# The half split behind the router, the last tile's chain first, and 15 warm-up matmuls in a fused attention, mixture-of-experts and SoLU kernel

## The chip, the cores and the metric

One core of a Trainium2 chip runs the whole program in one launch. The metric is the device time of one execution, in microseconds, as the median of several runs. An instruction belongs to one of five engines with a queue of its own: TensorE (PE: matmuls, with PEld for its weight loads), VectorE (DVE), ScalarE (ACT), GpSimd (POOL) and SyncE (SP, which issues transfers). Each engine takes its instructions in program order, and they wait for one another through semaphores.

## The reference

Three parts follow one another. The first is a gated linear attention with a stabilised recurrence, for 2 batches of 8 heads, 768 steps and head width 40:

```
m_new = max(f + m, i);  f_s = exp(f + m - m_new);  i_s = exp(i - m_new)
C = f_s * C + i_s * v k^T;   n = f_s * n + i_s * k
y = sigmoid(o) * (C q) / max(|n . q|, 1)
```

Its output is 1536 tokens of width 320. The second part sends each token to two of eight experts:

```
noisy = x @ w_gate + log1p(exp(x @ w_noise)) * noise
top2  = the two largest of noisy;  weights = softmax over the two
out  += weight * (relu(x @ w1[e]) @ w2[e])          # 320 -> 1024 -> 320
```

The third is a dense layer: h = x @ w_in, a softmax over h times h, a layer norm with gain g_ln, and a product with w_out (320 to 1024 to 320).

## The kernel before

**Stages.** The tokens are 12 tiles of 128; the batches alternate (`order`). Stage 1 (to about line 800) is the attention in chunks of 128 steps together with the routing. Then come the experts one after the other, and then the SoLU layer. Matrix products of the experts run as sums of a high part, rounded to the fast matmul format, and a low part, the remainder: for each weight ACT makes the high part (`split_hi`, L116) and DVE or POOL subtracts it from the raw weight (`split_lo`, L120).

**Order.** The schedule is manual: the order in which the program is written is the order on each engine. `weave` takes several short chains of DVE steps and writes one step of each in turn.

**The head.** `gates(0, 1)` (L268 to L285) runs two scans on DVE for the first chunk. G holds the sums of the log gates. Its high part goes to rows 0 to 15 of GP (L281), its low part to rows 32 to 47 (L282). `sel` (L297) is a selection matrix taken from the constants, in the fast format. `decays` multiplies sel by GP on PE (tile D, L307). Ahead of that, 20 matmuls of 448 columns on a constant tile `warm` (L253) keep PE busy; they write pw. Meanwhile POOL clears buffers (L240). ACT computes the sigmoid of the first two output gates (og_s, L298).

**A round of the loop** (i = 4 to 10, L678 to L717) works on four tiles at once. PE: ranks of tile i-3 (L452), scores of i+1 (tile S, L343), update of the state with i (tile U, L371), the part of i that goes through the state (L379), attend of i (tile Y, L384), transposes of i-1 (`trans`, tile pT, L418) and the router's logits (L428). DVE: the weave, made of `rows(i-1)` (normalise, x, L404 to L408; copy, L412), `route(i-2)` (top two of the noisy logits, one-hot oh, mask mk, running counts cum, L441 to L448) and `slot(i-3)` (row of each token in the experts' buffer, L458 to L460); then `probs` (E times S, L347, two halves), `keys` (kw, L360) and `state` (CC, L394). ACT: exponentials, and copies of pT (`transc`, L422). POOL: `send(i-3)` scatters the tile's tokens to their experts' rows in memory (xg, L476, an indirect transfer, two for each tile), then the causal mask on E (`causal`, L336), the queries' weighting (qa, L353) and the state's (CC, L355). From i = 5 on, DVE makes in each round one half of one of expert 0's first three low weights: w0l = r - w0h, 128x512, L703, **the half split**, behind probs(i+1, 1) and ahead of the next weave.

**The tail** (L722 to L798) handles tile 11, which is t. The first 192 rows of expert 0 are final by then, and the program starts on them: `early_turn` transposes them (ept, L506), `early_split` makes their high and low parts, `early_mm(f)` is layer 1 for one block of 128 hidden columns, eight matmuls (eph, L126 to L133). `split2(j)` makes one more low weight on DVE (L120) and loads another (r). `busy(n)` writes n matmuls on `warm`, as the warm-ups. When the last tile is sent, SP loads the rest of expert 0's rows (`rest`), and the expert stage turns them (L924).

Of the kernel before, what the change touches and what calls it, by code (L numbers as in the profile page):

```python
# [8 lines left out]
F32 = mybir.dt.float32  # L9
# [12 lines left out]
P = 128  # L22
# [14 lines left out]
def fused_kernel(ctx: ExitStack, tc, qt, kt, kv, og, ig, fg, wgn, noise, w1, w2, win, wout, gln, cst, out):  # L37
# [157 lines left out]
    with ExitStack() as pa:  # L195
# [53 lines left out]
            ve.memset(Kb[0][j], 0.0)  # L249
        ve.memset(Qb[0], 0.0)  # L250
        pw = ps1.tile([P, 512], F32, tag="U", name="pw")
        for i in range(20):
            pe.matmul(pw[:, 0:448], warm[:, 0:P], warm, start=True, stop=True)  # L253

        def fill(n, tag="U"):
# [12 lines left out]
        def gates(c0, c1):  # L268
            lo, hi = c0 * P, c1 * P
            m0, m1 = M[:, lo:hi], M[:, lo + 1 : hi + 1]  # L270
            Fs, Is, Gs = F[:, lo:hi], I[:, lo:hi], G[:, c0:c1].rearrange("p c t -> p (c t)")
            yield ve.tensor_tensor_scan(m1, Fs, Is, -1e30 if c0 == 0 else M[:, lo : lo + 1], ALU.add, ALU.max)
            if c0 == 0:
                ve.tensor_sub(M[:, 0:1], M[:, 1:2], F[:, 0:1])
            yield ve.tensor_add(Fs, Fs, m0)
            yield ve.tensor_sub(Fs, Fs, m1)
            yield ve.tensor_tensor_scan(Gs, R1[:, 0 : c1 - c0].rearrange("p c t -> p (c t)"), Fs, 0.0, ALU.mult, ALU.add)
            if c1 > 2:
                act.dma_start(gd[:, max(2, c0) * P : hi], G[:, max(2, c0) : c1].rearrange("p c t -> p (c t)"))
            if c0 < 2:  # L280
                yield ve.tensor_copy(GP[0:16, c0], G[:, c0])  # L281
                yield ve.tensor_sub(GP[32:48, c0], G[:, c0], GP[0:16, c0].bitcast(F32))  # L282
            yield ve.tensor_sub(Is, Is, m1)
            yield ve.tensor_sub(Is, Is, Gs)
            yield ve.tensor_add(BE[:, c0:c1], Iv[:, c0:c1], G[:, c0:c1, P - 1 : P].to_broadcast([16, c1 - c0, P]))  # L285
# [6 lines left out]
            ve.tensor_copy(bT[:, c0:c1], pb[:, 0, c0:c1])  # L292
            act.activation(wS[:, c0:c1], pb[:, 1, c0:c1], AF.Exp)

        for k, _ in enumerate(gates(0, 1)):
            if k == 3:
                ve.tensor_copy(sel, consts[0:48, 2 * P + 24 : 2 * P + 40])  # L297
        act.activation(og_s[:, 0:2], og_s[:, 0:2], AF.Sigmoid)  # L298
        act.preload_act_table_set("natural_log_exp_and_others")

# [80 lines left out]
        def attend(i, lo=0, hi=NH):  # L381
            b, c = order[i]
            for h in range(lo, hi):
                pe.matmul(T[i]["Y"][:, h], T[i]["E"][:, h], values(i)[:, h], start=(c == 0 and h == 0), stop=(h == NH - 1))  # L384
# [13 lines left out]
        def rows(i):  # L398
            Y = T[i]["Y"]
            den = a2.tile([P, NH, 1], F32, tag="den", name=f"den{i}")  # L400
            nm = a2.tile([P, NH, HD], F32, tag="nm", name=f"nm{i}")
            xx = T[i]["x"] = a4.tile([P, XR + 1], F32, tag="x", name=f"x{i}")
            pool.tensor_copy(xx[:, 384:385], tokid[:, i : i + 1])
            yield ve.tensor_scalar(den, Y[:, :, 40:41], -1.0, 1.0, op0=ALU.mult, op1=ALU.max)  # L404
            yield ve.tensor_mul(nm, Y[:, :, 0:HD], og_s[:, i].rearrange("p (h d) -> p h d", d=HD))
            yield ve.tensor_max(den, den, Y[:, :, 40:41])
            yield ve.reciprocal(den, den)
            yield ve.tensor_mul(xx[:, 0:DM].rearrange("p (h d) -> p h d", d=HD), nm, den.to_broadcast([P, NH, HD]))  # L408

        def rows2(i):  # L410
            xx = T[i]["x"]
            yield ve.tensor_copy(xx[:, DM:384], xx[:, 256:DM])  # L412

        def trans(i):
            pT = T[i]["pT"] = ps1.tile([P, 4, P], F32, tag="pT" if i < NTILE - 1 else "U", name=f"pT{i}")
            for k in range(3):
                w = min(P, DM - k * P)
                pe.transpose(pT[:w, k], T[i]["x"][:, k * P : k * P + w], ident)  # L418

        def transc(i):  # L420
            xT = T[i]["xT"] = a2.tile([P, 3, P], F32, tag="xT", name=f"xT{i}")
            act.activation(xT[:, 0:2], T[i]["pT"][:, 0:2], AF.Copy)  # L422
            act.activation(xT[0:64, 2], T[i]["pT"][0:64, 2], AF.Copy)
# [11 lines left out]
        def route(i):  # L435
            z = T[i]["z"]
            ix = a2.tile([P, 8], U32, tag="ix", name=f"ix{i}")
            ixf = T[i]["x"][:, 385:387]
            oh = T[i]["oh"] = a2.tile([P, 2, NE], F32, tag="oh", name=f"oh{i}")
            mk = T[i]["mk"] = a2.tile([P, NE], BF16, tag="mk", name=f"mk{i}")  # L440
            yield ve.tensor_mul(z, T[i]["pT"][:, 3, 32:40], noise_s[:, i])  # L441
            yield ve.tensor_add(z, z, T[i]["pT"][:, 3, 0:8])
            yield ve.max(V8[:, i], z)
            yield ve.max_index(ix, V8[:, i], z)
            yield ve.tensor_copy(ixf, ix[:, 0:2])
            yield ve.tensor_tensor(oh, ixf.rearrange("p (k o) -> p k o", o=1).to_broadcast([P, 2, NE]), iota8.rearrange("p (k e) -> p k e", k=1).to_broadcast([P, 2, NE]), op=ALU.is_equal)
            yield ve.tensor_add(mk, oh[:, 0], oh[:, 1])
            yield ve.tensor_add(cum[i + 1], cum[i], mk)  # L448
# [6 lines left out]
        def slot(i):  # L455
            sk = a2.tile([P, 2, NE], F32, tag="sk", name=f"sk{i}")
            sf = a2.tile([P, 2], F32, tag="sf", name=f"sf{i}")
            yield ve.tensor_mul(sk, T[i]["oh"], T[i]["pr"].rearrange("p (k e) -> p k e", k=1).to_broadcast([P, 2, NE]))  # L458
            yield ve.tensor_reduce(sf, sk, axis=AX.X, op=ALU.add)
            yield ve.tensor_copy(slots[:, i], sf)  # L460

        def weave(*chains):

            chains = list(chains)
            while chains:
                chains = [c for c in chains if next(c, chains) is not chains]
# [21 lines left out]
        def when(f, i, *a):  # L488
            if 0 <= i < NTILE:
                f(i, *a)  # L490
# [35 lines left out]
        def busy(n, tag="D"):  # L526
            w = ps1.tile([P, 448], F32, tag=tag, name="busy")
            for _ in range(n):
                pe.matmul(w, warm[:, 0:P], warm, start=True, stop=True)
# [148 lines left out]
        for i in range(4, NTILE - 1):  # L678
            when(load_qk, i + 3)
            when(load_kv, i + 2)  # L680
            ranks(i - 3)
            route_act(i - 2)
            weave(chain(rows(i - 1), rows2(i - 1)), route(i - 2), slot(i - 3))
            when(exps, i + 2)
            scores(i + 1, 0, 0, 2)
            update(i)
            scores(i + 1, 0, 2, 4)
            probs(i + 1, 0)
            keys(i + 1)
            if i > CUT + 1:  # L690
                send(i - 3)
            if i < CUT + 2:
                send(i - 3)
            inter(i)
            state(i)
            attend(i, 0, 2)
            scores(i + 1, 1, 0, 2)
            attend(i, 2, 5)
            scores(i + 1, 1, 2, 4)
            probs(i + 1, 1)  # L700
            if i > 4:
                j, hs = (i - 5) // 2, slice((i - 5) % 2 * 512, (i - 5) % 2 * 512 + 512)
                ve.tensor_sub(splits[0][1][:, j, hs], raws[0, j][:, 0, hs], splits[0][0][:, j, hs].bitcast(F32))  # L703
            trans(i - 1)
            transc(i - 1)
            attend(i, 5, 8)
            when(load_d, i + 4)
            when(causal, i + 2)
            logits(i - 1)
            for j in (i - 2,) if i < 7 else (5, 6) if i == 7 else ():  # L710
                load_w(0, j)
            for j in (i - 4,) if i < 8 else (4, 5) if i == 8 else (6,) if i == 9 else ():
                split_hi(0, j)
            if i == CUT + 2:
                early_load()
            for j in ((0, 1), (2,))[i - CUT - 1] if i > CUT else ():
                load_w(1, j)  # L717
        def split2(j):
            split_lo(0, j, ve)
            load_w(1, j)  # L720
# [6 lines left out]
        inter(t)  # L727
        weave(chain(rows(t - 1), rows2(t - 1)))
        attend(t, 0, 3)
        trans(t - 1)  # L730
        transc(t - 1)
        attend(t, 3)
# [7 lines left out]
        route_act(t - 1)  # L740
        weave(rows(t), slot(t - 2))
        send(t - 2)
        for d in range(3):
            early_turn(d)
            early_split(d)
        busy(2, "U")
        trans(t)
        transc(t)
        weave(route(t - 1))
        early_mm(0)  # L750
        logits(t)
        route_act(t)
        ranks(t - 1)
        early_mm(1)
        weave(slot(t - 1))
        send(t - 1)
        split2(3)
        early_mm(2)
        weave(rows2(t), route(t))
        early_mm(3)  # L760
        ranks(t)


        pn = ps1.tile([P, NE], F32, tag="pT", name="pn")
# [571 lines left out]
```

## Time and profile before

| | |
|---|---|
| runs of the kernel before | 434.88, 435.88 and 437.14 us, median 435.88 |
| the profiled execution | 435.03 us, span 433.4 us |
| mean granted clock of PE | 0.975 |
| busy: PE, DVE, ACT, POOL | 421.1, 298.3, 242.5, 196.4 us |

The profile gives one execution. Busy time is the sum over an engine's instructions. The granted clock is a share of full speed, so 0.5 means the lower of PE's two levels. The waits of an engine are put down to the instruction of another that released it last. The order of instructions, shown with the change, says nothing of time.

### The profile page before, as it was taken

The page shows a single profiled execution, that of the slowest core. Times are in us where ns is not written, and L with a number is a line of the kernel's source. Part 1 is how long each engine was busy: PE and PEld are TensorE (multiplying, and loading weights), DVE is VectorE, ACT ScalarE, POOL GpSimd, SP SyncE. Part 2 cuts the span into 40 slices and gives each one's busy share as a digit, 9 for nine tenths or more (in the row PEclk, how much of TensorE's full clock was granted, in tenths as well). Part 3 has the DMA queues.
Part 4 walks back from the last instruction along what each step waited for, and adds up shares of the span by engine and source line. Part 5 has one row for each costly group of instructions (what it writes and reads, how often), then busy time and mean ns, then how long its engine had stood idle before and what let it go on. Part 6 is the DMA issues. An engine that isn't in the chain of part 4 may idle for free.

```text
span 433.4 us, 8131 instructions
## 1 busy us (share of the span) xinstructions
PE 421.1 (97%) x2732; PEld 391.1 (90%) x2732; DVE 298.3 (69%) x754; ACT 242.5 (56%) x524; POOL 196.4 (45%) x281
## 2 busy tenths in 40 slices
PE   8999989999989999999999999999999999999996
PEld 4898978987989899899999999999896898999996
DVE  8896699994755467596685967756656875666541
ACT  3795957722246562645727456473735856655651
POOL 7582797654436443624536254452022543423230
PEclk9998999995899999999999999999999999999999
DMA  6888998924546758384683857637015012210001
GB/s 186 250 240 253 317 320 225 312 91 150 174 144 217 279 191 282 105 281 155 208 287 117 259 178 239 215 98 205 32 63 171 31 45 66 72 47 15 32 16 54
DMA packets 37536, 71.74 MB, mean 166 GB/s; under 512 B 4385, under 2 KB 19141, under 8 KB 37488
## 3 DMA queue, kind: packets, MB, share of 16 engines
q1 hardware_dynamic: 34336, 62.06, 46.0%
q0 software_dynamic: 2912, 8.68, 5.4%
q8 instruction: 24, 0.39, 0.4%
q10 hardware_dynamic: 240, 0.41, 0.3%
q14 instruction: 24, 0.20, 0.1%
HBM read 55.50 MB, written 16.21 MB: 165 GB/s over the span
## 4 chain that ended last, share of the span: by engine, by line
PE 80%; DVE 13%; DMA 3%; issue 2%; ACT 1%; POOL 0%; POOLq 0%; DVEq 0%; ACTq 0%
PE po L149 6%; PE po L148 6%; PE po L150 6%; PE ph L126 4%; PE cpo L1099 3%; PE cpo L1098 3%; PE cpo L1097 3%; PE ph L127 3%; PE ph L129 3%; PE ph L131 3%; PE ph L133 3%; PE ph L132 3%; PE ph L128 3%; PE ph L130 3%; PE pt L924 3%; DMA xg<-x,slots 2%
## 5 line engine op out<-in xcount | busy, mean ns | idle before, releaser
L165 POOL DMA_INDIRECT yt<-YS,ti x29 | 31.4, 1082 | 86.6 <-ACT YS L163 55.3
L139 DVE SCALAR_TENSOR_TENSOR h<-ph,h 128x384 fp32r<-128x384 f32 (+1 forms) x64 | 34.6, 541 | 51.4 <-ACT h L138 51.1
L120 POOL TENSOR_TENSOR w0l<-r,w0h 128x1024 fp32r<-128x1024 f32 x21 | 50.4, 2400 | 30.4 <-ACT w0h L116 30.1
L148 PE MATMUL po<-w1h,h 128*128 128x320 f32 x184 | 56.7, 308 | 0.0
L150 PE MATMUL po<-w1h,h 128*128 128x320 f32 x184 | 56.7, 308 | 0.0
L149 PE MATMUL po<-w1l,h 128*128 128x320 f32 x184 | 56.6, 308 | 0.0
L138 ACT ACTIVATE h<-ph 128x448 fp32r<-128x448 f32 (+6 forms) x64 | 32.1, 502 | 36.3 <-PE ph L133 29.6
L476 POOL DMA_INDIRECT xg<-x,slots x24 | 25.6, 1066 | 21.6 <-DVE slots L460 5.6
L149 PEld LDWEIGHTS po<-w1l,h 128*128 128x128 f32 x184 | 34.6, 188 | 0.0
L148 PEld LDWEIGHTS po<-w1h,h 128*128 128x128 f32 x184 | 34.5, 188 | 0.0
L150 PEld LDWEIGHTS po<-w1h,h 128*128 128x128 f32 x184 | 34.5, 188 | 0.0
L343 PE MATMUL S<-Qb,Kb 128*128 128x128 f32 x192 | 30.7, 295 | 0.7 <-DVE E L347 0.7
L120 DVE TENSOR_TENSOR w1l<-r,w1h 128x640 fp32r<-128x640 f32 x36 | 29.4, 820 | 2.5 <-ACT w1h L116 2.5
L1091 DVE TENSOR_TENSOR ZL<-pz,ZH 128x512 fp32r<-128x512 f32 x24 | 15.4, 685 | 22.6 <-ACT ZH L1090 22.6
L1097 PE MATMUL cpo<-w1h,ZH 128*128 128x320 f32 x96 | 29.8, 311 | 0.0
L1099 PE MATMUL cpo<-w1h,ZL 128*128 128x320 f32 x96 | 29.6, 308 | 0.0
L163 ACT ACTIVATE YS<-po 128x320 f32<-128x320 f32 x20 | 8.8, 438 | 37.2 <-issue 31.1
L1098 PE MATMUL cpo<-w1l,ZH 128*128 128x320 f32 x96 | 29.6, 308 | 0.0
L116 ACT ACTIVATE w0h<-r 128x1024 fp32r<-128x1024 f32 x27 | 28.2, 1050 | 0.0
L343 PEld LDWEIGHTS S<-Qb,Kb 128*128 128x128 f32 x192 | 25.4, 199 | 1.3 <-DVE E L347 1.1
L384 PE MATMUL Y<-KV,E 128*128 128x41 f32 x192 | 25.6, 279 | 0.0
L116 ACT ACTIVATE w1h<-r 128x640 fp32r<-128x640 f32 x36 | 25.4, 730 | 0.0
(263 smaller groups left out, 1248.0 us busy)
## 6 DMA issues: line engine op xcount, KB each, us to landing
r<-in_w_dram SPq DMA_DIRECT2D x24, 512.0 KB
r<-in_w_dram SPq DMA_DIRECT2D x32, 320.0 KB
E<-gd SPq DMA_DIRECT2D x8, 512.0 KB
X<-xg SPq DMA_DIRECT2D x7, 579.0 KB
KV<-in_kv_dram SPq DMA_DIRECT2D x12, 324.0 KB
cY<-yt SPq DMA_DIRECT2D x12, 320.0 KB
cvR<-in_win_dram SPq DMA_DIRECT2D x6, 512.0 KB
cvR<-in_wout_dram SPq DMA_DIRECT2D x5, 512.0 KB
```

What stands on the lines that cost most here:

```text
L116: act.activation(splits[e][2 * m][:, k : k + n], raws[e, j], AF.Copy)
L120: eng.tensor_sub(splits[e][2 * m + 1][:, k : k + n], raws[e, j], splits[e][2 * m][:, k : k + n].bitcast(F32))
L138: act.activation(h[:, 0:n], ph, AF.Relu)
L139: ve.scalar_tensor_tensor(h[:, n + r : n + r + w], ph[:, 0:w], 0.0, h[:, 0:w].bitcast(F32), op0=ALU.max, op1=ALU.subtract)
L148: pe.matmul(po, hh, W2H[:, f], start=a, stop=False)
L149: pe.matmul(po, hh, W2L[:, f], start=False, stop=False)
L150: pe.matmul(po, hl, W2H[:, f], start=False, stop=z)
L165: i = pool.indirect_dma_start(out=yt, out_offset=bass.IndirectOffsetOnAxis(ap=idx[0:w], axis=0), in_=YS[0:w], in_offset=None, bounds_check ...
L343: pe.matmul(S[:, a], Kb[i % 3][j][:, a], Qb[i % 3][:, a], start=True, stop=True)
L1097: pe.matmul(po, ZH[:, f], W2H[:, f], start=(f == 0), stop=False)
L1098: pe.matmul(po, ZH[:, f], W2L[:, f], start=False, stop=False)
L1099: pe.matmul(po, ZL[:, f], W2H[:, f], start=False, stop=(f == 7))
```

## The change

Four edits. The number of warm-ups is 15. ACT casts `sel`, now ahead of the gates, and the high part of G for the first chunk. In the loop the half split stands right behind the weave. In the tail `trans(t)` and `transc(t)` go ahead of the early turns, `split2(3)` and `logits(t)` behind the weave of route(t-1), early_mm(0) behind ranks(t-1), `rows2(t)` and `route(t)` ahead of early_mm(2), and ranks(t) ahead of early_mm(3); two busy matmuls are added ahead of trans(t-1).

```diff
--- before.py
+++ after.py
@@ -249,7 +249,7 @@
             ve.memset(Kb[0][j], 0.0)
         ve.memset(Qb[0], 0.0)
         pw = ps1.tile([P, 512], F32, tag="U", name="pw")
-        for i in range(20):
+        for i in range(15):
             pe.matmul(pw[:, 0:448], warm[:, 0:P], warm, start=True, stop=True)
 
         def fill(n, tag="U"):
@@ -278,7 +278,7 @@
             if c1 > 2:
                 act.dma_start(gd[:, max(2, c0) * P : hi], G[:, max(2, c0) : c1].rearrange("p c t -> p (c t)"))
             if c0 < 2:
-                yield ve.tensor_copy(GP[0:16, c0], G[:, c0])
+                yield act.activation(GP[0:16, c0], G[:, c0], AF.Copy) if c0 == 0 else ve.tensor_copy(GP[0:16, c0], G[:, c0])
                 yield ve.tensor_sub(GP[32:48, c0], G[:, c0], GP[0:16, c0].bitcast(F32))
             yield ve.tensor_sub(Is, Is, m1)
             yield ve.tensor_sub(Is, Is, Gs)
@@ -292,9 +292,9 @@
             ve.tensor_copy(bT[:, c0:c1], pb[:, 0, c0:c1])
             act.activation(wS[:, c0:c1], pb[:, 1, c0:c1], AF.Exp)
 
-        for k, _ in enumerate(gates(0, 1)):
-            if k == 3:
-                ve.tensor_copy(sel, consts[0:48, 2 * P + 24 : 2 * P + 40])
+        act.activation(sel, consts[0:48, 2 * P + 24 : 2 * P + 40], AF.Copy)
+        for _ in gates(0, 1):
+            pass
         act.activation(og_s[:, 0:2], og_s[:, 0:2], AF.Sigmoid)
         act.preload_act_table_set("natural_log_exp_and_others")
 
@@ -681,6 +681,9 @@
             ranks(i - 3)
             route_act(i - 2)
             weave(chain(rows(i - 1), rows2(i - 1)), route(i - 2), slot(i - 3))
+            if i > 4:
+                j, hs = (i - 5) // 2, slice((i - 5) % 2 * 512, (i - 5) % 2 * 512 + 512)
+                ve.tensor_sub(splits[0][1][:, j, hs], raws[0, j][:, 0, hs], splits[0][0][:, j, hs].bitcast(F32))
             when(exps, i + 2)
             scores(i + 1, 0, 0, 2)
             update(i)
@@ -698,9 +701,6 @@
             attend(i, 2, 5)
             scores(i + 1, 1, 2, 4)
             probs(i + 1, 1)
-            if i > 4:
-                j, hs = (i - 5) // 2, slice((i - 5) % 2 * 512, (i - 5) % 2 * 512 + 512)
-                ve.tensor_sub(splits[0][1][:, j, hs], raws[0, j][:, 0, hs], splits[0][0][:, j, hs].bitcast(F32))
             trans(i - 1)
             transc(i - 1)
             attend(i, 5, 8)
@@ -727,6 +727,7 @@
         inter(t)
         weave(chain(rows(t - 1), rows2(t - 1)))
         attend(t, 0, 3)
+        busy(2, "U")
         trans(t - 1)
         transc(t - 1)
         attend(t, 3)
@@ -740,25 +741,25 @@
         route_act(t - 1)
         weave(rows(t), slot(t - 2))
         send(t - 2)
+        busy(2, "U")
+        trans(t)
+        transc(t)
         for d in range(3):
             early_turn(d)
             early_split(d)
-        busy(2, "U")
-        trans(t)
-        transc(t)
         weave(route(t - 1))
-        early_mm(0)
+        split2(3)
         logits(t)
         route_act(t)
         ranks(t - 1)
+        early_mm(0)
         early_mm(1)
         weave(slot(t - 1))
         send(t - 1)
-        split2(3)
+        weave(rows2(t), route(t))
         early_mm(2)
-        weave(rows2(t), route(t))
+        ranks(t)
         early_mm(3)
-        ranks(t)
 
 
         pn = ps1.tile([P, NE], F32, tag="pT", name="pn")
```

ACT at its beginning, as the difference (- before, + after); sel and GP are the two casts, og_s the sigmoid:

```order
 L247 ACT_TABLE_LOAD
+L295 ACTIVATE sel<-consts 48x16
+L281 ACTIVATE GP<-G 16x128
 L298 ACTIVATE og_s<-og_s 128x640
 L299 ACT_TABLE_LOAD
```

The two casts stand ahead of the sigmoid and its table load; on DVE both are gone, and L282 follows the scan directly.

DVE in round i = 5, before; from the end of one weave (cum) to the beginning of the next (den):

```order
L447 TENSOR_TENSOR mk_849<-oh_848 128x8
L448 TENSOR_TENSOR cum_86<-cum_85,mk_849 128x8
L347 TENSOR_TENSOR E_596<-E_596,S_0_879 128x512
L360 TENSOR_TENSOR kw_155<-KV_728,wS 128x4x40 x2
L394 TENSOR_TENSOR CC_161<-CC_161,U_882 40x4x41 x2
L347 TENSOR_TENSOR E_596<-E_596,S_1_908 128x512
L703 TENSOR_TENSOR w0l_243<-r_0_600,w0h_242 128x512
L404 TENSOR_SCALAR den_949<-Y_899 128x8
```

The same place after:

```order
L447 TENSOR_TENSOR mk_844<-oh_843 128x8
L448 TENSOR_TENSOR cum_86<-cum_85,mk_844 128x8
L686 TENSOR_TENSOR w0l_238<-r_0_595,w0h_237 128x512
L347 TENSOR_TENSOR E_591<-E_591,S_0_875 128x512
L360 TENSOR_TENSOR kw_155<-KV_723,wS 128x4x40 x2
L394 TENSOR_TENSOR CC_161<-CC_161,U_878 40x4x41 x2
L347 TENSOR_TENSOR E_591<-E_591,S_1_904 128x512
L404 TENSOR_SCALAR den_944<-Y_895 128x8
```

The half split (now L686) moved from behind the second probs, L347, to ahead of the first; numbers of buffers differ by the five warm-ups that went.

PE in the tail, before, from the first early turn (ept) on; x_1511 is the last tile's, so L418 here is trans(t):

```order
L506 MATMUL ept_1527<-consts,eX 128x128
L506 MATMUL ept_1527<-consts,eX 128x64
L506 MATMUL ept_1532<-consts,eX 128x128
L506 MATMUL ept_1532<-consts,eX 128x64
L506 MATMUL ept_1537<-consts,eX 128x128
L506 MATMUL ept_1537<-consts,eX 128x64
L529 LDWEIGHTS warm
L529 MATMUL busy<-warm 128x448
L529 LDWEIGHTS warm
L529 MATMUL busy<-warm 128x448
L418 MATMUL pT_1546<-consts,x_1511 128x128 x2
L418 MATMUL pT_1546<-consts,x_1511 64x128
```

Behind these come the eight matmuls of early_mm(0), then logits(t) (L428), then ranks(t-1) (L452). The same place after; x_1509 is the last tile's, and pr_1571 is ranks(t-1):

```order
L418 MATMUL pT_1528<-consts,x_1509 128x128 x2
L418 MATMUL pT_1528<-consts,x_1509 64x128
L506 MATMUL ept_1535<-consts,eX 128x128
L506 MATMUL ept_1535<-consts,eX 128x64
L506 MATMUL ept_1540<-consts,eX 128x128
L506 MATMUL ept_1540<-consts,eX 128x64
L506 MATMUL ept_1545<-consts,eX 128x128
L506 MATMUL ept_1545<-consts,eX 128x64
L428 MATMUL pT_1528<-wgn_s,xT_1532 128x16 x3
L452 LDWEIGHTS ltri
L452 MATMUL pr_1571<-mk_1553,ltri 128x8
```

trans(t) moved ahead of the turns (the two busy matmuls stand ahead of it), and logits(t) and ranks(t-1) follow the turns with no early_mm between.

## Rows read from the trace of the kernel before

**Rows 1.** The page: the chain that ended last, by engine.
```profile
PE 80%; DVE 13%; DMA 3%; issue 2%; ACT 1%; POOL 0%; POOLq 0%; DVEq 0%; ACTq 0%
```

**Rows 2.** Stretches: us, then busy of PE, PEld, DVE, ACT, POOL; PEclk, DMA, GB/s.
```profile
70.00:80.00 10.00, 9.34 (x69) 9.00 (x69) 9.82 (x43) 5.48 (x17) 6.81 (x10) 0.83 0.89 289
...
71.00:72.00 1.00, 0.37 (x4) 0.37 (x4) 0.97 (x6) 0.00 (x0) 0.84 (x1) 1.00 0.87 304
...
95.00:115.00 20.00, 19.39 (x114) 17.07 (x113) 12.43 (x69) 5.28 (x20) 8.43 (x18) 0.66 0.42 127
...
96.00:97.00 1.00, 0.64 (x7) 0.52 (x5) 0.97 (x6) 0.00 (x0) 0.00 (x0) 1.00 0.00 0
...
200.00:300.00 100.00, 100.00 (x623) 97.34 (x622) 70.91 (x151) 54.70 (x96) 45.43 (x41) 1.00 0.60 191
```

**Rows 3.** Waits of PE, 0 to 125 us: in total, times, longest.
```profile
PE pT L418 <- DVE x L445: 1.5, 2, 0.8
...
PE pt L924 <- DMA rest<-xg: 1.4, 1, 1.4
...
PE S L343 <- DVE E L347: 0.7, 2, 0.5
...
PE pT L418 <- DVE slots L460: 0.6, 1, 0.6
```

**Rows 4.** Timeline, 0 to 8 us: start, duration, engine, line; idle before it.
```profile
1.95 5.86 PE L253 MATMUL pw<-warm 128*128 128x448 bf16 x20 [1.95 <-DVE warm L235]
...
5.08 2.21 DVE L297 CAST sel<-consts 48x16 fp32r<-48x16 f32 x1
...
5.13 0.74 ACT L298 ACTIVATE og_s<-og_s 128x640 f32<-128x640 f32 x1 [1.99 <-DMA og_s<-in_og_dram]
5.25 2.10 DVE L281 CAST GP<-G 16x128 fp32r<-16x128 f32 x1
...
5.66 1.71 PEld L253 LDWEIGHTS <-warm 128*128 128x128 bf16 x9 [0.22 <-issue]
...
7.38 0.28 DVE L282 TENSOR_TENSOR GP<-G,GP 16x128 fp32r<-16x128 f32 x1
```

**Rows 5.** Line 703: duration ns min/median/max, first and last start.
```profile
L703 DVE TENSOR_TENSOR w0l<-r,w0h x6: 683/2762/2876, 59.5 to 94.5; 128x512 fp32r<-128x512 f32 x6
```

**Rows 6.** Timeline of the loop, DVE and POOL.
```profile
54.90 1.29 DVE L412 COPY x<-x 128x64 f32<-128x64 f32 x1
...
64.04 0.19 DVE L412 COPY x<-x 128x64 f32<-128x64 f32 x1
...
65.23 0.57 DVE L360 TENSOR_TENSOR kw<-KV,wS 128x160 f32<-128x160 f32 x2
...
66.19 1.11 POOL L336 TENSOR_SCALAR_AFFINE_SELECT E<-E 128x1024 f32<-128x1024 f32 x1
...
67.02 2.88 DVE L703 TENSOR_TENSOR w0l<-r,w0h 128x512 fp32r<-128x512 f32 x1
...
68.60 0.73 POOL L355 TENSOR_TENSOR CC<-CC,A 128x328 f32<-128x328 f32 x1
...
93.86 0.97 POOL L476 DMA_INDIRECT xg<-x,slots  x1 [0.21 <-issue]
...
94.48 0.68 DVE L703 TENSOR_TENSOR w0l<-r,w0h 128x512 fp32r<-128x512 f32 x1
```

**Rows 7.** The tail: chain of waits (start, us, what), and two timeline rows.
```profile
101.14 2.10 PE ept L506 x6
...
106.72 1.26 PE pT L428 x6
...
108.64 0.82 DVE L120 TENSOR_TENSOR w1l<-r,w1h 128x640 fp32r<-128x640 f32 x1
...
112.47 0.18 PE L452 MATMUL pr<-mk,ltri 128*128 128x8 bf16 x1
...
118.99 3.79 DMA rest<-xg
```

## The prediction

> **What bounds the kernel now.** I read the chain of waits by engine first: TensorE (PE) carries 80% of it, VectorE (DVE) 13%, transfers 3% [rows 1]. Then I cut the span into stretches. In the middle of the expert stage PE is busy 100.00 of 100 us [rows 2]; there nothing but PE sets the time, so whatever lets that stage start earlier is kept to the end, one for one. The gaps lie before about 125 us, and the table of waits of PE for that stretch has the large ones: 1.5 us of trans (L418) waiting for DVE's routing chain, 0.7 of scores (L343) for probs (L347), 0.6 of trans for the slots of a tile, 1.4 of the first expert's turn (L924) for the rest of its rows [rows 3]. That is little. The clock costs more: its mean is 0.83 in 70 to 80 us and 0.66 in 95 to 115 us [rows 2]. [...] At the head of both stretches PE had a hole: it worked 0.37 of the microsecond from 71, and 0.64 of the one from 96 [rows 2]. So a short wait of PE is paid twice, by itself and in the clock behind it.
>
> **The head.** The 20 warm-up matmuls end at 1.95 + 5.86 = 7.81 us, and the last nine are 1.71 / 9 = 0.19 us apart, at the full clock [rows 4]. The gate sums are ready by 7.38 + 0.28 = 7.66, so the warm-ups end last, by little. Five fewer end at 7.81 - 5 x 0.19 = 6.86. DVE would not be ready then: its casts of sel and GP took 2.21 and 2.10 us for 16 columns and 128 columns, beside POOL's memsets. The change gives both to ScalarE (ACT), idle for 1.99 us until 5.13 when its first activation starts [rows 4]. The trace has no such cast on ACT; its price lies between nothing and the 0.74 of that 128x640 activation. Even at 0.74 each, sel from 5.08, GP from 5.82, they end at 6.56, and DVE's low part (0.28) at 6.84, still before 6.86. The sigmoid behind them on ACT comes up to 1.5 later, its gates are first read by rows(0), far behind. **Term: -0.95**; bounds 0 (an ACT price that only moves the wait) and -0.95, since PE is the next limit.
>
> **The loop.** Six times the half split (L703, 128x512) stands on DVE: 0.683 us at the least, 2.762 in the median, 2.876 at most [rows 5]. Its cause is beside it: queued at 67.02, it waits through POOL's L336 (66.19, 1.11), L353 and L355 (68.60 + 0.73 = 69.33) and ends at 69.90, 0.57 after the last; the one that took 0.68 stood beside an indirect transfer (L476) on POOL and nothing else [rows 6]. So the stall is 2.76 - 0.68 = 2.1 us a round, and behind it stand the weave's rows, routing and slots, for which PE's trans waits. The new place, between weave and probs, lies beside L476, where the row says 0.68. Of the waits in [rows 3], 1.5 + 0.7 us are the loop's. The rest of the stall is hidden by PE's own work. I take **-2.0**, ends 0 and -2.2.
>
> What is late next: POOL's L336, L353 and L355 now fall beside the weave. In a round without a split the copy L412 took 1.29 at 54.90, against 0.19 in another round [rows 6], 1.1 more. That is half of what the split loses, so DVE gains a microsecond in most rounds.
>
> [...]
>
> Without the hole at 71, the dip of 3.4 us in 70 to 80 (worth 3.4 / 2 = 1.7 us of PE time) may go, or be set off by another hole. Half of it: **-0.8**, ends 0 and -1.7.
>
> **The tail.** Order on PE before: three early turns (2.10 us of the chain from 101.14), busy, trans(t), early_mm(0), logits(t) at 106.72, and ranks(t) only at 112.47; the last scatter lets the transfer of the rest go at 118.99 [rows 7]. Moving trans(t) and logits(t) forward takes about the turns' 2 us out of the router's front. But three early_mm now stand ahead of ranks(t) too, DVE's split2(3), 0.82 [rows 7], goes in front of slot(t-1), and route(t-1) waits for the three early splits as before. At the same clock I make that zero: the end of the tail is PE's own work, most of which only changes places, and only 1.4 us of waiting [rows 3] is there to be had.
>
> The gain comes if the clock stays up. The hole of 96 to 97 is just where the added busy(2, "U") stands, ahead of trans(t-1), so PE is no longer idle there. The added two matmuls fill idle time; were they not to, they cost 2 x 0.19 us by [rows 4], 2 x 0.38 at the low clock. What is late next is ranks(t-1): nothing covers it now that early_mm(0) comes after it, while DVE still has three early splits and eight routing instructions to do. I put that hole at 0 to 2 us, the nearest row being the 2.10 of the turns whose splits it waits for. It can set off a dip of its own, and I take that as long as the one in the loop, 3.4 us. Then PE gets back (13.6 - 3.4) / 2 = 5.1 us. Half of it reaches the end, since routing, scatter and transfers do not run by PE's clock: **-2.5**, ends 0 and -13.6 / 2 = -6.8.
>
> **Sum.** -0.95 - 2.0 - 0.8 - 2.5 = -6.25. On the profiled execution, 435.03 us with its span of 433.4, that is 428.8; the median of the runs, 435.88, stands 0.85 above the profiled one, so the forecast is 429.6.
>
> **Rivals.**
> - All clocks stay up: the hole before ranks(t-1) sets off nothing and the loop's dip goes whole. -0.95 - 2.0 - 1.7 - 3.4 (half of 6.8) = -8.05: 427.8. For it: each dip has its own hole in the trace, both filled. Against: the new hole. 0.16.
> - The tail's clock falls as long as before, from the new hole, and the loop's too: only -0.95 - 2.0 are left, 432.9. For it: the clock was 0.66 there although PE was busy 19.39 of the 20 us [rows 2]. 0.22.
> - The stall only moves. POOL's block meets the weave, at 1.1 or more a round, the holes of PE remain, and the dips with them. The head alone: 434.9. For it: 54.90 [rows 6]. Against: the rows in which the split waited out three instructions. 0.10.
> - Slower: the key weighting kw (L360) is held instead. Its second half ended 65.23 + 0.57 = 65.80, L336 began at 66.19 [rows 6]; the margin is 0.39, and the split ahead of it pushes it by 0.68, past that point. If L336 comes first and kw then starves until L355's end at 69.33, as the split did, there follow 0.28 of kw and the instructions that stood between 65.73 and 67.02, 1.3 us: the weave begins at 70.9 instead of 69.90. That is 1.0 a round in i = 5 to 8 (kw is not made after that), 4.0 in all, with the holes and dips as before: 435.88 - 0.95 + 4.0 = 438.9. It decides from a kw that issues after L336; if POOL is delayed with it, since its own block waits for the same things, it does not. 0.07.
> - The forecast's own case: 0.45, by itself 428 to 431.5.
>
> The range goes from 427.0, between the first rival and the bounds below it, to 434.5, which leaves out the slower case, most of the stall that moves, and the far end of the clocks. About 0.5% of 435.88, 2.2 us, is what a measurement of this kernel can tell from no change: faster is below 433.7, slower above 438.06. Faster: 0.45 + 0.16 + most of 0.22 = 0.80; within: the 0.10 and the rest, 0.13; slower 0.07.
>
> **What would show it.** In the profile after: the first D matmul (L307) at about 6.9; the half split near 0.7 us in its six places, and no wait of trans for L445 of more than a few tenths; the clock in 70 to 80 above 0.83; in 95 to 115 above 0.8, with the fall after a hole before ranks(t-1) if there is one; the transfer of the rest going out by about 113 instead of 118.99. The forecast is wrong if the clock in the tail is as low as before, if L412, L446 or L360 take over a microsecond where L703 did, or if D waits for GP.

## The result and the profile after

The changed kernel is slower: 441.21 us in the median of 20 runs (436.41 to 447.52) against 436.9 (431.81 to 442.85, 20 runs); ratio 1.0102, interval 1.0077 to 1.0128. The forecast, 429.6 with 427.0 to 434.5, had the sign wrong. The profiled execution has a span of 437.6 us against 433.4, and a mean clock of 0.959 against 0.975. Runs of one kernel mostly spread over 2 to 3% here; a ratio compares the runs near each kernel's fastest, so where a kernel's spread is wide the ratio of the medians stands beside it.

The local steps came as foretold. The head's rows on TensorE, the scalar and the vector engine (start, duration, engine, line), the answer to [rows 4]:

```profile
1.95 4.93 PE L253 MATMUL pw<-warm 128*128 128x448 bf16 x15 [1.95 <-DVE warm L235]
...
4.55 0.22 ACT L295 ACTIVATE sel<-consts 48x16 fp32r<-48x16 f32 x1 [1.41 <-DMA consts<-in_cst_dram]
5.23 0.31 ACT L281 ACTIVATE GP<-G 16x128 fp32r<-16x128 f32 x1 [0.46 <-DVE G L277]
5.57 0.28 DVE L282 TENSOR_TENSOR GP<-G,GP 16x128 fp32r<-16x128 f32 x1 [0.44 <-ACT GP L281]
...
6.82 1.10 PE L307 MATMUL D<-GP,sel 48*128 48x128 f32 x8
```

The casts took 0.22 and 0.31 us, the low part was ready at 5.85, and D began at 6.82, right behind the warm-ups. All six half splits took 0.684 (the view of one line, duration min/median/max in ns), against a median of 2.762 [rows 5]:

```profile
L686 DVE TENSOR_TENSOR w0l<-r,w0h x6: 684/684/685, 56.1 to 94.7; 128x512 fp32r<-128x512 f32 x6
```

But the waits of TensorE moved (same view as [rows 3]: total, times, longest):

```profile
PE S L343 <- DVE E L347: 1.4, 2, 1.2
PE pr L452 <- DVE mk L447: 1.1, 1, 1.1
PE pT L418 <- DVE x L408: 0.9, 1, 0.9
PE pT L418 <- DVE den L406: 0.8, 1, 0.8
```

The wait of trans for L445 (1.5) is gone. Scores now wait 1.4 for probs instead of 0.7, and the tail has two waits that it did not have, 0.9 of trans(t) for x and 1.1 of ranks(t-1). The stretches of the profile show what followed (us, then busy of PE, PEld, DVE, ACT, POOL, the granted clock, DMA). After:

```profile
30.00:40.00 10.00, 9.15 (x83) 8.57 (x83) 7.25 (x32) 6.14 (x19) 2.46 (x4) 1.00 0.83 255
50.00:60.00 10.00, 8.75 (x67) 8.18 (x66) 7.56 (x30) 8.59 (x25) 9.38 (x14) 0.85 0.98 325
...
56.00:57.00 1.00, 0.27 (x3) 0.11 (x2) 0.97 (x4) 0.88 (x4) 1.00 (x1) 1.00 0.82 297
...
60.00:70.00 10.00, 10.00 (x50) 9.89 (x50) 8.52 (x20) 1.79 (x5) 6.99 (x11) 0.50 0.44 161
70.00:80.00 10.00, 9.97 (x73) 9.80 (x74) 8.61 (x34) 6.34 (x19) 5.63 (x8) 0.79 0.72 216
95.00:115.00 20.00, 17.95 (x116) 16.18 (x115) 12.04 (x59) 4.87 (x19) 7.89 (x17) 0.75 0.42 138
103.00:104.00 1.00, 0.23 (x2) 0.26 (x3) 0.59 (x2) 0.00 (x0) 0.73 (x1) 1.00 0.22 85
...
115.00:130.00 15.00, 15.00 (x94) 14.95 (x94) 8.96 (x43) 3.79 (x12) 2.09 (x4) 0.77 0.51 165
```

Of before, three stretches that [rows 2] does not have:

```profile
30.00:40.00 10.00, 9.85 (x76) 8.81 (x74) 6.53 (x31) 6.09 (x20) 1.90 (x4) 0.83 0.75 240
...
33.00:34.00 1.00, 1.00 (x7) 0.91 (x7) 0.94 (x3) 0.21 (x1) 0.00 (x0) 0.58 0.22 72
...
115.00:130.00 15.00, 13.20 (x101) 12.46 (x99) 9.43 (x40) 5.52 (x15) 4.35 (x6) 1.00 0.58 182
```

The scattering of the last tile ended later, not earlier: the transfer of the rest of expert 0's rows (`rest`) went out at 122.2 us, against 118.99 before [rows 7].

In both traces the clock is 1.00, or 0.50 inside the low stretches (60 to 70 above), so the time at the lower clock is (1 - clock) x length / 0.5. After: 3.0 + 10.0 + 4.2 + 10.0 + 6.9 = 34.1 us, in two stretches. Before: 3.4 + 3.4 + 13.6 = 20.4 in three. The 13.7 more cost TensorE about 13.7 / 2 = 6.9 us; the half is an estimate, from the matmuls of attend in the trace after: six took 0.35 us more than four at clock 0.50 (1.34 at 64.36, 0.99 at 62.58), and 0.18 more at 1.00 (0.76 at 75.39, 0.58 at 74.46). The span grew by 4.2, so everything else became 2.7 us shorter, near the -0.95 and -2.0 of the sum. What was forecast as a gain of 3.3 by the clock (-0.8 and -2.5) came as a loss of 6.9. One execution is one draw, but span and mean clock are known for every run. By the same sum over whole spans the changed kernel was at the lower clock for 36.5 us in the mean of its 20 runs, the kernel before for 24.1 in the 168 runs taken beside the experiments; the span less half of that time is 421.5 against 423.2. So over all runs, too, the clock cost more (12.4 / 2 = 6.2 us) than the rest gave back (1.7).

Ahead of both stretches after the change TensorE had a hole: it worked 0.27 of the microsecond from 56, and 0.23 of the one from 103. A hole and a fall do not always go together, though: after the change TensorE also stood for 0.85 us at 33 and the clock stayed at 1.00 (30 to 40 above), while before it fell just there with TensorE busy for the whole of that microsecond.

One more row was late. The key weighting (kw, L360) took 0.57 for both halves before [rows 6]. Timeline of DVE and POOL in round i = 6 of the changed kernel:

```profile
63.95 3.23 DVE L360 TENSOR_TENSOR kw<-KV,wS 128x160 f32<-128x160 f32 x2
...
64.31 1.10 POOL L336 TENSOR_SCALAR_AFFINE_SELECT E<-E 128x1024 f32<-128x1024 f32 x1
...
65.50 1.26 POOL L353 TENSOR_TENSOR qa<-Qb,A 128x512 f32<-128x512 f32 x1
```

The split, 0.68 ahead of it, pushed its second half past the start of L336, and it ended only after L353 had, at 66.76: kw starved. That is the slower rival's mechanism, twice here (2.83 us in the next round). In this execution TensorE was at half clock there and did not wait for it; two of the experiments show it in the open.

### The profile page after: what moved, and what is told of

Its sections match the earlier page's. It is cut to its first block, busy times and chain, and to the rows that moved or that the text cites. A ratio compares the mean times of both kernels' runs of the same rounds, so it can differ in the third digit from the quotient of the medians.

```text
span 437.6 us, 8125 instructions
## 1 busy us (share of the span) xinstructions
PE 425.4 (97%) x2729; PEld 397.8 (91%) x2729; DVE 293.7 (67%) x752; ACT 242.8 (55%) x526; POOL 195.2 (45%) x281
## 4 chain that ended last, share of the span: by engine, by line
PE 89%; DVE 7%; DMA 1%; issue 1%; ACT 0%; POOL 0%; DVEq 0%; ACTq 0%
PE po L148 6%; PE po L149 6%; PE po L150 6%; PE S L343 4%; PE ph L126 3%; PE Y L384 3%; PE cpo L1100 3%; PE cpo L1098 3%; PE cpo L1099 3%; PE ph L127 3%; PE ph L129 3%; PE ph L133 3%; PE ph L131 3%; PE ph L132 3%; PE ph L128 3%; PE ph L130 3%
## 5 line engine op out<-in xcount | busy, mean ns | idle before, releaser
L120 POOL TENSOR_TENSOR w0l<-r,w0h 128x1024 fp32r<-128x1024 f32 x21 | 50.4, 2400 | 30.4 <-ACT w0h L116 30.1
L476 POOL DMA_INDIRECT xg<-x,slots x24 | 25.3, 1052 | 25.2 <-DVE ix L444 9.5
L343 PE MATMUL S<-Qb,Kb 128*128 128x128 f32 x192 | 32.6, 307 | 1.4 <-DVE E L347 1.4
L343 PEld LDWEIGHTS S<-Qb,Kb 128*128 128x128 f32 x192 | 26.9, 209 | 1.9 <-DVE E L347 1.7
L384 PEld LDWEIGHTS Y<-KV,E 128*128 128x128 f32 x192 | 25.7, 204 | 0.2
```

The costliest lines, as they stand in the source:

```text
L120: eng.tensor_sub(splits[e][2 * m + 1][:, k : k + n], raws[e, j], splits[e][2 * m][:, k : k + n].bitcast(F32))
L343: pe.matmul(S[:, a], Kb[i % 3][j][:, a], Qb[i % 3][:, a], start=True, stop=True)
```

## The experiments

| kernel | ratio to before, interval | ratio of medians |
|---|---|---|
| head alone | 0.9995, 0.9946 to 1.0044 | 1.0024 |
| loop alone | 1.0027, 0.9989 to 1.0064 | 1.0008 |
| tail alone | 1.0054, 1.0021 to 1.0088 | 1.0033 |
| changed, first split old | 1.0115, 1.0059 to 1.0172 | 1.0152 |
| changed, busy in round 5 | 1.0055, 1.0011 to 1.0099 | 1.0042 |
| changed, tail covered | 1.0018, 0.9982 to 1.0053 | 0.9989 |
| changed, split behind kw | 1.0134, 1.0074 to 1.0194 | 1.0122 |
| before, holes filled | 0.9990, 0.9953 to 1.0028 | 0.9987 |
| changed, round 5 and tail | 1.0066, 1.0022 to 1.0111 | 1.0106 |
| tail alone, early_mm(0) first | 1.0008, 0.9967 to 1.0050 | 0.9979 |
| splits late, new tail covered | 0.9897, 0.9852 to 0.9943 | 0.9958 |
| splits late, old tail | 0.9940, 0.9901 to 0.9978 | 0.9935 |
| changed, splits late | 0.9984, 0.9939 to 1.0029 | 1.0022 |
| before, splits late | 0.9957, 0.9920 to 0.9995 | 0.9989 |
| changed, kw on POOL | 0.9957, 0.9917 to 0.9997 | 1.0044 |
| changed, kw on POOL, tail covered | 1.0029, 0.9982 to 1.0076 | 1.0077 |
| splits late, kw on POOL, tail covered | 1.0044, 1.0006 to 1.0082 | 1.0021 |
| changed, busy in round 6 | 1.0038, 0.9994 to 1.0082 | 1.0071 |

**One part at a time.** Each takes its lines of the change alone, and the fourth puts only the first half split back:

```diff
             probs(i + 1, 1)
+            if i == 5:
+                half_split(i)
```

> The kernel before with the head's edits alone (15 warm-ups, both casts on the scalar engine). Theory 1 (the half split ahead of probs makes a hole on TensorE in round i = 5, and the clock falls behind it): the head gives its 1.0 us and nothing else, ratio about 0.998. Theory 2 (the tail's new order costs): the same 0.998. Theory 3 (the shorter head shifts where the clock falls, and that is what made it slower): 1.005 or more.

> The kernel before with the half split moved alone. Theory 1: the hole at 57 us and a fall of the clock of some 16 us behind it (8 us of TensorE's time), less the 2 us of waits that go: ratio 1.008 to 1.014, clock of 60 to 70 us near 0.5. Theories 2 and 3: faster than before by 2 us or more, ratio 0.995 or less.

> The kernel before with the tail's new order alone. Theory 1: no change, ratio 0.997 to 1.003, since the clock falls in the tail of before as well, for 13.6 us there and 16 in the changed kernel. Theory 2: ranks(t-1), with nothing to cover it, waits 1.1 us, and the tail is 3 to 4 us later: ratio 1.008.

> The changed kernel with the first of the six half splits (i = 5) back in its old place, behind the second probs; the other five stay in the new one. Theory 1: the wait of scores for probs falls from 1.2 to 0.5 us, the clock stays up from 58 to 74 us, ratio to before 0.990 to 0.995. Theories 2 and 3: as the changed kernel, 1.007 to 1.012.

No part explains the loss by itself; the three add to 1.0076. The loop's 2 us did not arrive, though its trace has the split at its short time (0.68 us), and the tail's order costs. Neither theory's range held for the loop or for the tail. Theory 1 in its narrow form fell: with the first split in its old place the wait of scores is 0.3 us, and the kernel is no faster. Its trace shows why. kw starves all the same, and with the clock up TensorE stands (one row of DVE, one of PE, of that kernel):

```profile
64.56 3.23 DVE L360 TENSOR_TENSOR kw<-KV,wS 128x160 f32<-128x160 f32 x2
...
68.43 0.81 PE L371 MATMUL U<-KV,kw 128*104 128x82 f32 x3 [2.77 <-DVE CC L394]
```

The update needs kw and the state, both queued behind it. The mean clock of that execution was 0.955 over 440.1 us, by the sum above 39.6 us at the lower clock.

**Covering holes.** Busy matmuls, or early_mm(0), where TensorE waits:

```diff
# e_fill5
+            if i == 5:
+                busy(6)
             when(exps, i + 2)
# e_filltail
-        busy(2, "U")
+        busy(6, "U")
         trans(t)
...
+        early_mm(0)
         logits(t)
         route_act(t)
         ranks(t - 1)
-        early_mm(0)
# b_fill: before, busy(4) ahead of scores (i = 5) and trans(i-1) (i = 5, 6), busy(3) ahead of trans(t-1)
# e_kwfirst: the changed kernel, the half split behind keys(i + 1)
```

> The changed kernel with six more busy matmuls (1.1 us at the full clock) on TensorE in round i = 5, between the weave and the scores, just where it waited 1.2 us for probs at 57 us. Theory A (the low stretches of the clock follow holes of TensorE): the stretch of 17 us from 57.6 is gone or begins later, at the next hole; 2 to 8 us faster than the changed kernel, ratio to before 0.992 to 1.006. Theory B (the clock falls whatever TensorE does): as the changed kernel, 1.010, or 0.5 us more. Theory C (the starved key weighting at 64 and 74 us is what costs): as the changed kernel, with kw (L360) at 2.8 us twice.

> The changed kernel with the two waits of its tail covered: six instead of two busy matmuls ahead of trans(t), and early_mm(0) ahead of logits(t) again, where ranks(t-1) waited 1.1 us. Theory A: the low stretch of 17 us from 104.9 is shorter or gone, 2 to 7 us faster than the changed kernel, ratio to before 0.993 to 1.005. Theories B and C: 1.010 as the changed kernel, within 0.003.

> The changed kernel with the half split behind keys(i+1) instead of ahead of probs(i+1, 0), so that kw (L360) and the first probs come as early as before. Theory C: no kw over 0.4 us, the split 0.7 us, and the hole in round i = 5 back to 0.5 us: 2 to 5 us faster than the changed kernel, ratio 0.998 to 1.005. Theory A alone: the hole of round i = 5 is smaller, that of the tail is not; 1.003 to 1.008. Theory B: 1.010.

> The kernel before with busy matmuls in the holes that TensorE had there: four ahead of the scores in round i = 5, four ahead of trans(i-1) in rounds i = 5 and 6, three ahead of trans(t-1). Theory A: fewer low stretches, 2 to 6 us faster than before, ratio 0.986 to 0.995. Theory B: 1.000 to 1.003, slower by what the matmuls cost where they do not fit the hole.

The tail's cover takes 0.84% off, and the waits of TensorE behind 95 us fall to 0.3 for L447 and 0.2. The split behind kw starved once itself (3.47 us), kw did once as well (2.82), and nothing was gained. Filling before's holes gave nothing measurable, and in its trace the clock fell all the same, for 13.6 us from 102, though TensorE had worked at least 0.85 of every microsecond from 73 on (columns as above):

```profile
100.00:101.00 1.00, 0.85 (x7) 0.61 (x6) 0.96 (x6) 0.36 (x2) 0.79 (x4) 1.00 0.86 234
...
102.00:103.00 1.00, 0.94 (x4) 0.26 (x5) 0.47 (x2) 0.71 (x3) 0.78 (x3) 0.67 0.86 346
```

So a hole as long as those above is not needed for a fall. In e_fill5 the matmuls ran at 51.9 us, a round too early: TensorE is in round 6 when the vector engine does round 5. So its expectation was put wrongly, and its better time settles nothing on the hole at 56.

**Both covers, and the splits elsewhere.**

```diff
# v_late_new, v_late_old (head and splits; the tails as named)
+            for n in (0, 1) if i == 9 else (2, 3) if i == 10 else ():   # behind the weave
+                half_split(n)
+            if i == 5:
+                busy(4)
...
+            for n in (4, 5) if i == 10 else ():                         # behind probs(i + 1, 1)
+                half_split(n)
```

> The changed kernel with both covers, that of round i = 5 (six busy matmuls) and that of the tail (four more busy matmuls ahead of trans(t), early_mm(0) ahead of logits(t)). Theory A (holes lower the clock, in both places): the two gains add, 1.0102 - 0.0047 - 0.0084 = 0.997, range 0.992 to 1.001. Theory B (the two shorter times were chance): 1.003 to 1.010. Theory C (the starved kw is the rest): not below 0.997, with kw at 3.2 us in two or three rounds.

> The kernel before with the tail's new order, but early_mm(0) ahead of logits(t), so that ranks(t-1) has work ahead of it as it had before. Theory A (the uncovered wait of ranks(t-1) is what the tail's order costs): 1.000 against 1.0054 with the new order whole. Rival (the wait of trans(t) for x, moved ahead of the turns, costs): 1.005 as that.

> A version: the changed kernel with both of the tail's waits covered, and the six half splits in rounds i = 9 (two) and 10 (four), where no kw follows and POOL's mask is over, with four busy matmuls in round i = 5. Theories A and C together: no split, kw or CC over 0.8 us in rounds 5 to 10, no low stretch of 17 us from 57; ratio 0.985 to 0.995. If only the clock's chance decides: 1.000 to 1.005.

> The same with the tail in the order of the kernel before, and three busy matmuls ahead of trans(t-1). Theory A: 0.985 to 0.997; against the version with the tail's new order this tells what that order is worth once its waits are covered: by the forecast 2.5 us faster with it, by the time of the tail's order alone the same within 0.003.

e_tail_mm0 points the same way for the tail: its new order with early_mm(0) ahead of logits(t) has no wait of ranks(t-1) at all, and 1.0008 in place of 1.0054, though the two intervals overlap. Both covers together missed 0.997 and gave 1.0066: three kw starved there (3.38, 3.24, 2.83 us). With the splits in rounds 9 and 10, where kw is no longer made, the versions are the fastest of all. In the trace with the old tail every pair of kw takes 0.55 to 0.57; in the one with the new tail, three take 1.5 to 1.8 us. The new tail, covered, is 0.4% ahead of the old one by the ratio and 0.2% behind by the medians, so its worth is not settled.

**Is it kw?**

```diff
# e_late_only: the changed kernel, splits late as above, no busy(4); b_late: the same in before
# e_kwpool
-                    (pool if i < 4 else ve).tensor_mul(kw
+                    (pool if i < 10 else ve).tensor_mul(kw
```

> The changed kernel with the six half splits in rounds i = 9 (two) and 10 (four) and nothing else changed: no added cover in round 5 or in the tail. Theory C (the split pushes kw into POOL's block, and kw starves): 0.993 to 1.000, no kw over 0.4 us in rounds 5 to 8. Theory A alone (only uncovered holes matter, and the tail's is left): 1.005 to 1.010.

> The kernel before with the six half splits late and nothing else changed. Theory C: the splits' stalls go and nothing starves in their place: 0.992 to 0.997. If the stalls were hidden by TensorE's work anyway: 0.998 to 1.002.

> The changed kernel with the split in its new place and the key weighting kw on GpSimd in all rounds (as it is for the first four tiles) instead of the vector engine. Theory C: nothing on the vector engine starves by kw; GpSimd gets 1.45 us more in each round and is then near full, so some of the gain is lost there: 0.998 to 1.005. Without theory C: 1.010 or more, since GpSimd's chain grows.

> The changed kernel with the key weighting on GpSimd in all rounds and the tail's waits covered (six busy matmuls ahead of trans(t), early_mm(0) ahead of logits(t)). If the two causes add: 0.9957 - 0.0084 = 0.987, range 0.983 to 0.992, near the forecast's own 0.986. If they do not add, since both act through the clock: 0.993 to 0.998.

> The version with the half splits late (0.9897 with kw on the vector engine), with the key weighting on GpSimd too. If a starved kw is left in that version in some runs: 0.983 to 0.988; if GpSimd's longer chain costs more than that: 0.990 to 0.994. Against v_kwpool_tail the same within 0.003 if the split's new place costs nothing by itself.

With the split out of kw's way, or kw off the vector engine, the changed kernel goes from 1.0102 to 0.9984 and 0.9957, by the medians from 1.0099 to 1.0022 and 1.0044. Both intervals lie clear of the changed kernel's, so the split's place ahead of kw is a part of the loss, worth between 0.6 and 1.5%. That it costs by starving kw is argued from the traces, not shown by the times. The split is not the only way into it: kw starved once in b_late (3.37 us at 64.51) and in e_tail_mm0 (3.11), and three times in e_head (2.61 to 2.82), none of which has the split in the new place; the margin ahead of L336 is small in any case (0.39 us in [rows 6]). And b_late, with the stalls of the old place gone, is ahead of before by the ratio but hardly by the medians.

With the tail covered as well, the two ways part. Late splits go on from 0.9984 to 0.9897 (with four busy matmuls in round 5), about the 0.84% of the cover. kw on POOL goes back from 0.9957 to 1.0029, where 0.987 was expected, and with the splits late too it is 1.0044, where 0.983 to 0.994 was. So the gains do not always add. With kw on POOL the vector engine waits elsewhere: x (L408), 0.45 to 0.50 us each time in before, takes 1.2 us three times in v_all and 2.55 once:

```profile
55.11 2.55 DVE L408 TENSOR_TENSOR x<-nm,den 128x320 f32<-128x320 f32 x1 [2.57 <-issue]
```

**The hole itself.** The last run puts busy(6) at i == 6, at the same line.

> The changed kernel with six more busy matmuls (1.1 us at the full clock) on TensorE in round i = 6, between the weave and the scores, in the hole of 56.3 to 57.5 us. If the hole lowers the clock: the stretch of 17 us from 57.6 is gone or shorter, then the starved kw shows on TensorE as a wait of 2 to 3 us for CC, ratio 1.000 to 1.007. If not: the stretch is there all the same, 1.008 to 1.013.

Stretches of this kernel, as above, then its timeline of PE, DVE and POOL:

```profile
56.00:57.00 1.00, 0.97 (x9) 0.85 (x7) 1.00 (x1) 1.00 (x3) 1.00 (x2) 1.00 0.93 367
57.00:58.00 1.00, 0.76 (x7) 0.55 (x8) 0.93 (x6) 0.89 (x4) 0.87 (x3) 1.00 0.79 303
58.00:59.00 1.00, 1.00 (x6) 0.30 (x4) 1.00 (x3) 0.97 (x2) 0.79 (x3) 1.00 1.00 302
...
60.00:61.00 1.00, 0.00 (x0) 0.00 (x0) 1.00 (x1) 1.00 (x5) 1.00 (x3) 1.00 1.14 346
61.00:62.00 1.00, 0.00 (x0) 0.00 (x0) 1.00 (x1) 0.52 (x2) 1.00 (x1) 0.96 1.09 388
62.00:63.00 1.00, 0.06 (x1) 0.07 (x1) 0.95 (x4) 0.00 (x0) 0.16 (x2) 0.50 0.98 370
...
70.00:80.00 10.00, 10.00 (x55) 9.89 (x55) 6.77 (x27) 5.47 (x15) 4.58 (x8) 0.55 0.57 170
```

```profile
57.72 0.68 DVE L686 TENSOR_TENSOR w0l<-r,w0h 128x512 fp32r<-128x512 f32 x1
57.73 1.30 PE L529 MATMUL busy<-warm 128*128 128x448 bf16 x6
...
58.92 3.39 DVE L360 TENSOR_TENSOR kw<-KV,wS 128x160 f32<-128x160 f32 x2
...
59.68 1.10 POOL L336 TENSOR_SCALAR_AFFINE_SELECT E<-E 128x1024 f32<-128x1024 f32 x1
...
60.87 1.25 POOL L353 TENSOR_TENSOR qa<-Qb,A 128x512 f32<-128x512 f32 x1
...
62.94 0.81 PE L371 MATMUL U<-KV,kw 128*104 128x82 f32 x3 [3.17 <-DVE CC L394]
```

This is the chain in one execution. The first hole is mostly filled, and the clock is still 1.00 up to 61. But now kw starves a round earlier than in the changed kernel (there this kw took 0.57 at 57.35), and in the open: 3.39 us, until L353 has ended at 62.12, and TensorE stands still for 3.17. The clock falls there and is at 0.50 for 17.1 of the next 18 us. Taking one hole away brought the next, and the low stretch with it. The time, 1.0038 by the ratio, lies in the range for "if the hole lowers the clock"; by the medians, 1.0071, it is at the edge of it.

## Why the prediction was wrong

- **The head (-0.95): right in place**, 0.99 us earlier at D. By the time, 0.9995 with half a per cent either way, it is neither shown nor refuted.
- **The split's own stall: right in size, but not in every round.** No split takes over 0.69 now; in before the stall had cost 2.0 to 2.2 us in four rounds, 1.5 in one and nothing in the last. The wait of trans for L445 went too. But the loop alone, 1.0027 with 0.9989 at the least, rules out the -2.0 (0.9954) that this was to bring.
- **What the split would do in its new place: wrong, the first failed step.** The sum took the new place, "beside L476, where the row says 0.68", as free for what stands behind it. But in before scores already waited 0.5 for probs there [rows 3]; the split stands ahead of that probs, and the wait became 1.2. And kw was priced as a rival, 1.0 a round with a chance of 0.07, from a margin of 0.39 that the shift of 0.68 overran by its own numbers. It happened in two or three rounds of every kernel whose trace is used here that kept all six splits ahead of probs and kw on the vector engine. The price was of the wrong kind too: TensorE's wait for the update varied from nothing (the changed kernel, at the low clock) over at most 1.0 us (e_fill5) to 2.77 and 3.17.
- **The clock: wrong, the step that set the sign.** The sum booked -0.8 in the loop and -2.5 in the tail, for holes filled; low stretches of 17.1 us came in both places. For the new hole the term was "I take that as long as the one in the loop, 3.4 us", although the tail's own stretch in the same trace was 13.6. Both figures are (1 - clock) x length / 0.5 on the stretches of [rows 2]; by the microsecond that trace has 3.4 us at 0.50 from 74 and 13.7 from 98. That vector work does not run by TensorE's clock, as the sum took it, holds here: the half split took 0.68 us at 0.50 (62.75) as at 1.00 (81.30). Beneath it lay the reading that "a short wait of PE is paid twice, by itself and in the clock behind it", from two stretches that had a hole ahead. The same trace has a stretch from 33 without one, and a hole of 0.85 us, the longer wait of trans for L445, with the clock at 1.00 behind it. In the traces low stretches last 3.4 us (before, from 74), 6.8 (e_fill5, from 106), 10.2 (e_filltail, from 108), 13.7 (before, from 98), 17.1 (after, from 57) and up to 27.3 (v_late_new, from 35). Where they end is not settled by any run here: after the change TensorE was busy 10.00 of 10 us from 60 and the clock stayed low.
- **The tail at the same clock: wrong by the new wait.** The hole ahead of ranks(t-1) was seen and bounded at 0 to 2 us (1.1 came, and 0.9 of trans(t) for x), but then given no price of its own. Covered, 0.84% comes back; the order alone, covered, is worth nothing measurable (1.0008).
- **What the split waited out: kw did the same.** The stall was taken from the case in which the split waited through L336, L353 and L355 [rows 6]. In the new place kw took 3.23 us where it met L336 and L353, and 0.57 where it ended ahead of them; L336 ended at 65.41, and kw waited on through L353. The third rival, a weave held at 1.1 us or more a round, came in one round of the trace after: the slots cast (L460) took 1.46 at 60.05, beside L353 and L355. L412's 1.29 stood in both traces.

What stays open: how the clock's stretches come about, and so why gains found one by one do not add. Nor does a run take the head alone out of the changed kernel; by the sum over all runs the head alone was at the lower clock for 30.1 us, before in the 35 runs beside it for 23.0, so a part of the loss may lie in the earlier start itself.

## What to carry over

A short operation moved ahead of a chain pushes everything queued behind it, and the price is read from the smallest margin there (0.39 us here), not from the operation's own time. Where the matrix engine's clock falls now and then, do not book a gain for a hole that is filled, since falls came here with and without holes; let the bounds of that term reach to the longest low stretch in the trace and not the shortest, compare the clock over many runs, and leave no wait uncovered that had work ahead of it. Six splits in two late rounds, away from what they collide with, beat both kernels: 0.9897 with the tail covered, 0.9940 with the old tail (each with four busy matmuls in round 5).

## What was not expected of the hardware

Two vector operations waited through several GpSimd instructions in a row: kw of 0.32 us a half took up to 3.39 us for the pair (e_fill6), the half split up to 2.88 instead of 0.68 [rows 6]. TensorE's clock stayed at 0.50 for 17.1 us although TensorE was busy without a gap for ten of them (60 to 70 us after the change). And it fell with hardly a hole ahead: at 33 us in before TensorE worked the whole microsecond, and ahead of the fall at 102 in before with its holes filled at least 0.85 of each.
